# One matmul per key tile for the sums of V and K, in a backward pass of cached attention, with a new on-chip layout

## The chip, the cores and the metric

The kernel runs on one core of a Trainium2 chip. The metric is device time in microseconds, the median of several executions; all of them below are in the same (fast) state or, where a program ran once only, of unknown state. Ratios are the mean time of one kernel's runs over the mean of the other's runs of the same rounds, so they are not quite the ratio of the medians that are quoted. The kernel before has some stragglers: 5 of its 34 executions took 801.8 to 802.7 us, and no trace shows one.

## The reference, cut to what matters

One decode step of a small layer (attention over the last 4,096 keys of a cache of 32,768, then a gated feed-forward block) and its gradients with respect to every input.

```python
W = min(4096, max(256, Sk // 4))                       # 4096 keys used, 28672 not
k = jnp.repeat(k_cache[:, :, Sk - W:, :], rep, axis=1) # 8 heads of 256, 16 query heads
v = jnp.repeat(v_cache[:, :, Sk - W:, :], rep, axis=1)
p = _softmax(jnp.einsum("bhqd,bhkd->bhqk", q, k) * (Dh ** -0.5), axis=-1)
o = jnp.einsum("bhqk,bhkd->bhqd", p, v)
# outputs: the step's result and the gradients, among them those of the whole
# k_cache and v_cache, [1, 8, 32768, 256] in bfloat16 each, 268 MB together
```

Seven eighths of the two cache gradients are zero and must be written as zeros. That is what most of the kernel's bytes are.

## The kernel before

A 16 KB block of zeros per partition is sent again and again ("fills") to the untouched rows. The fills go out on the GpSimd queue in two batches. The second batch waits until the upper half of the zero block, which holds a block of feed-forward weights in between, is cleared again.

```python
HALF0, HALF1 = 42, 55          # 42 fills from 16 KB, 13 from its lower 8 KB read twice
send_fills(0, HALF0)
send_fills(HALF0, HALF1, True)
# ... cut: the attention forward stage, feed-forward blocks 0 and 1 ...
            if n == 1:
                nc.vector.memset(ar(ZW // 2, ZW // 2), 0.0)     # L426
                send_fills(HALF1, len(fills))                   # 48 more, from L427
```

In the forward stage each head g has its scores, then its "moments": the products p V^T K for the gradient of q (M_ps), and the sums of V and of K with the probabilities (ok_ps). These last are what the change touches:

```python
            for c in range(8):
                pK = pK_slot[c % 2]
                nc.vector.tensor_tensor(out=pK, in0=K_sb[:, 4*c:4*c+4, :]..., in1=p_f..., op=ALU.mult)   # L304
                for i in range(4):
                    for vh in range(2):
                        nc.tensor.matmul(M_ps[:, vh, :], lhsT=V_sb[:, t, ...], rhs=pK[:, i]...)          # L309
            for k, X_sb in enumerate((V_sb, K_sb)):
                for t in range(T):                                                                       # T = 32
                    nc.tensor.matmul(ok_ps[:, k, :], lhsT=ppad[...], rhs=X_sb[:, t, :], ...)             # L313
```

All big buffers are offsets in one arena: six regions of 16 KB for V, a region MB of 32 KB for the moments, and a region RB of 50 KB for K, the working slots and, after the stage, the output and feed-forward weights.

Of the kernel before, what the change touches and what calls it, by code (L numbers as in the profile page):

```python
# [15 lines left out]
H = 16  # L16
G = 8
Dh = 256
W = 4096
T = 32  # L20
# [9 lines left out]
KB = 512  # L30
# [3 lines left out]
def kernel(  # L34
        ctx, tc, A_x, A_k_cache, A_v_cache, A_wq, A_wo, B_x, B_w_gate, B_w_up, B_w_down, grad_out,
           out_0, out_1, out_2, out_3, out_4, out_5, out_6, out_7, out_8):
    nc = tc.nc
# [7 lines left out]
    ps_t = ctx.enter_context(tc.tile_pool(name="ps_t", bufs=1, space=bass.MemoryType.PSUM))  # L45

    VB = 16 * KB
    MB = VB + 6 * 16 * KB
    RB = MB + 32 * KB
    TOTAL = RB + 50 * KB  # L50
    arena = const.tile([128, TOTAL], bf16)

    def ar(off, n):
        return arena[:, off:off + n]

    def kv_at(off):
        return ar(off, T * Dh).rearrange("p (t d) -> p t d", d=Dh)

    zeros = ar(0, ZW)
    A_off = [VB + 16 * KB * i for i in range(6)]  # L60
    V_off = [A_off[i] for i in (0, 1, 2, 3, 4, 5, 0, 1)]
    K_off = [RB, RB + 16 * KB, MB + 16 * KB, RB, RB + 16 * KB, A_off[1], RB, RB + 16 * KB]
    M_sb = [ar(MB + 4 * KB * g, 4 * KB).bitcast(f32).rearrange("p (v h d) -> p v h d", v=2, h=2) for g in range(G)]
    wqA = ar(MB, 24 * KB).rearrange("p (c j) -> p c j", c=3)
    wqB = ar(MB + 24 * KB, 4 * KB)
    KT_slot = [ar(RB + (32 + 2 * i) * KB, 2 * KB).rearrange("p (e t k) -> p e t k", t=4, e=2) for i in range(3)]
    pK_slot = [ar(RB + (38 + 4 * i) * KB, 4 * KB).rearrange("p (t h d) -> p t h d", t=4, h=2) for i in range(2)]
    ppad = [ar(RB + (46 + i) * KB, T * H).rearrange("p (t h) -> p t h", h=H) for i in range(2)]
    rows1 = ar(RB + 48 * KB, 2 * KB)[0:16].bitcast(f32)
    ok_rows = ar(RB + 48 * KB, 2 * KB)[0:H].bitcast(f32).rearrange("p (k d) -> p k d", k=2)  # L70

# [123 lines left out]
    def load_kv(off, cache, g):  # L195
        LD.dma_start(out=kv_at(off), in_=cache[0, g, Sk - W:, :].rearrange("(p t) d -> p t d", t=T))
# [21 lines left out]
    for c in range(16):  # L218
        nc.tensor.matmul(qT_ps[:, c::16], lhsT=wqB[:, c * 128:(c + 1) * 128], rhs=X1_b[:, 3:5], start=True, stop=False)
        for h in range(2):  # L220
            col = 16 * h + c
            for k in range(3):
                nc.tensor.matmul(qT_ps[:, col:col + 1], lhsT=wqA[:, k, col * 128:(col + 1) * 128], rhs=X1_b[:, k:k + 1],
                                 start=False, stop=(h == 1 and k == 2))
# [14 lines left out]
    def fill_vpad(i, src):  # L239

        nc.vector.tensor_copy(out=vpad[i][:].rearrange("p e (c w) -> p e c w", w=18)[:, :, :, 0:2],
                              in_=src.unsqueeze(2).to_broadcast([128, 2, 8, 2]))
# [19 lines left out]
    with tc.tile_pool(name="ps_m", bufs=1, space=bass.MemoryType.PSUM) as ps_m, \  # L262
            tc.tile_pool(name="ps_x", bufs=1, space=bass.MemoryType.PSUM) as ps_x, \
            tc.tile_pool(name="ps_c", bufs=1, space=bass.MemoryType.PSUM) as ps_c, \
            tc.tile_pool(name="work1", bufs=2) as work1:

        def scores(g):
            fill_vpad(g % 2, qT_bf[:, 4 * g:4 * g + 4].rearrange("p (k e) -> p e k", e=2))
            sT_ps = dots(kv_at(K_off[g]), KT_slot, vpad[g % 2], rows1, ps_c, "cols", lambda q, XT, ps: nc.scalar.copy(out=XT, in_=ps))  # L269
            pmax = small.tile([16, 1], f32, tag="pmax")  # L270
            nc.vector.reduce_max(out=pmax[:], in_=rows1, axis=AX)
            pmaxT_ps = ps_t.tile([1, 16], f32, tag="tmp")
            nc.tensor.transpose(pmaxT_ps[:], pmax[:], ident_f[0:16, 0:16])
            gmax = small.tile([1, 2], f32, tag="gmax")
            nc.vector.reduce_max(out=gmax[:], in_=pmaxT_ps[:].rearrange("o (c h) -> o h c", h=2), axis=AX)
            nc.vector.tensor_scalar(out=gmax[:], in0=gmax[:], scalar1=-SCALE, scalar2=None, op0=ALU.mult)
            nb_ps = ps_t.tile([128, 2], f32, tag="tmp")
            nc.tensor.matmul(nb_ps[:], lhsT=ones_f[0:1, 0:128], rhs=gmax[:], start=True, stop=True)
            nbias = small.tile([128, 2], f32, tag="nbias")
            nc.vector.tensor_copy(out=nbias[:], in_=nb_ps[:])  # L280
            e_f = work1.tile([128, T, 2], f32, tag="e_f")
            psums = small.tile([128, 2], f32, tag="psums")
            for hh in range(2):
                nc.scalar.activation(out=e_f[:, :, hh], in_=sT_ps[:].rearrange("p i c h -> p (i c) h")[:, :, hh], func=ACT.Exp, bias=nbias[:, hh:hh + 1], scale=SCALE,  # L284
                                     accum_out=psums[:, hh:hh + 1])
            tot_ps = ps_t.tile([128, 2], f32, tag="tmp")
            nc.tensor.matmul(tot_ps[:], lhsT=ones_f[:, :], rhs=psums[:], start=True, stop=True)
            rsum = small.tile([128, 2], f32, tag="rsum")
            nc.vector.reciprocal(out=rsum[:], in_=tot_ps[:])
            nc.vector.tensor_tensor(out=pT_all[:, g], in0=e_f[:], in1=rsum[:].unsqueeze(1).to_broadcast([128, T, 2]), op=ALU.mult)  # L290
            p_f = work1.tile([128, T, 2], f32, tag="p_f")
            nc.vector.tensor_copy(out=p_f[:], in_=pT_all[:, g])
            pp = ppad[g % 2]
            if g > 1:
                nc.vector.memset(pp[:, :, 2 * g - 4:2 * g - 2], 0.0)
            nc.vector.tensor_copy(out=pp[:, :, 2 * g:2 * g + 2], in_=pT_all[:, g])  # L296
            return p_f

        def moments(g, p_f):
            K_sb, V_sb = kv_at(K_off[g]), kv_at(V_off[g])  # L300
            M_ps = ps_m.tile([128, 2, 2 * Dh], f32, tag="M")
            for c in range(8):
                pK = pK_slot[c % 2]
                nc.vector.tensor_tensor(out=pK, in0=K_sb[:, 4 * c:4 * c + 4, :].unsqueeze(2).to_broadcast([128, 4, 2, Dh]),  # L304
                                        in1=p_f[:, c::8, :].unsqueeze(3).to_broadcast([128, 4, 2, Dh]), op=ALU.mult)
                for i in range(4):
                    t = 4 * c + i
                    for vh in range(2):
                        nc.tensor.matmul(M_ps[:, vh, :], lhsT=V_sb[:, t, vh * 128:(vh + 1) * 128], rhs=pK[:, i, :, :].rearrange("p h d -> p (h d)"),  # L309
                                         start=(t == 0), stop=(t == T - 1))  # L310
            for k, X_sb in enumerate((V_sb, K_sb)):
                for t in range(T):
                    nc.tensor.matmul(ok_ps[:, k, :], lhsT=ppad[g % 2][:, 8 * (t % 4) + t // 4, :], rhs=X_sb[:, t, :],  # L313
                                     start=(g == 0 and k == 0 and t == 0), stop=(g == G - 1 and k == 1 and t == T - 1))
            for vh in range(2):
                nc.scalar.copy(out=M_sb[g][:, vh].rearrange("p h d -> p (h d)"), in_=M_ps[:, vh, :])

        def load_wo(n):
            LD.dma_start(out=wo_sb[:, 16 * n:16 * n + 16, :], in_=A_wo.rearrange("(p j) n -> p j n", j=32)[:, 16 * n:16 * n + 16, :])

        ok_ps = ps_x.tile([H, 2, Dh], f32, tag="ok")
        after = {0: [("K", 3), ("V", 3)], 1: [("K", 4), ("V", 4), ("K", 5)], 2: [("V", 5)], 3: [("V", 6), ("K", 6)], 4: [("K", 7)], 5: [("V", 7)]}
        p_next = scores(0)
        for g in range(G):
            p_f = p_next
            if g + 1 < G:
                p_next = scores(g + 1)
            moments(g, p_f)
            for kind, n in after.get(g, []):
                if kind == "K":  # L330
                    load_kv(K_off[n], A_k_cache, n)
                else:
                    load_kv(V_off[n], A_v_cache, n)
            if g == G - 2:
                load_wo(0)
        nc.vector.tensor_copy(out=ok_rows, in_=ok_ps[:])
# [151 lines left out]
    with tc.tile_pool(name="work2", bufs=2) as work2, tc.tile_pool(name="lnw", bufs=1) as lnw, \  # L488
            tc.tile_pool(name="ps_d", bufs=2, space=bass.MemoryType.PSUM) as ps_d:
        for g in range(G):  # L490
            dqb_ps = ps_d.tile([128, 2, 512], f32, tag="d", name="dqb_ps")
            for hh in range(2):
                h = 2 * g + hh
                for vh in range(2):
                    nc.tensor.matmul(dqb_ps[:, 0, hh * Dh:(hh + 1) * Dh], lhsT=doT_f[:, vh, h:h + 1].to_broadcast([128, 128]), rhs=M_sb[g][:, vh, hh, :],  # L495
                                     start=(vh == 0), stop=False)
                for kh in range(2):
                    nc.tensor.matmul(dqb_ps[:, 0, hh * Dh + kh * 128:hh * Dh + (kh + 1) * 128], lhsT=ndk[:, kh, h:h + 1].to_broadcast([128, 128]), rhs=ident_f[:],  # L498
                                     start=False, stop=(kh == 1))
            nc.scalar.activation(out=dq_bc[:, g * 512:(g + 1) * 512], in_=dqb_ps[:, 0, :], func=ACT.Copy, scale=SCALE)  # L500
        for g in range(2):
            load_kv(MB + 16 * KB * g, A_v_cache, g)

# [94 lines left out]
        for it, g in enumerate(order):  # L598
            V_sb = kv_at(V2_off[it])
# [31 lines left out]
            for l in range(8):  # L631
                for qp in range(2):
                    d_ps = ps_d.tile([128, 2, 2, Dh], f32, tag="d")
                    for qi in range(2):
                        q = 2 * qp + qi
                        nc.tensor.matmul(d_ps[:, qi].rearrange("p w d -> p (w d)"), lhsT=rT[32 * q:32 * (q + 1), :], rhs=RB_[32 * q:32 * (q + 1), l, :],  # L636
                                         start=True, stop=True)
                    t = 4 * l + 2 * qp
# [47 lines left out]
```

## Time and profile before

| | before |
|---|---|
| median of 3 executions before the prediction | 799.91 us |
| span of the profiled execution | 798.2 us |
| bytes moved by DMA | 334.80 MB, mean 419 GB/s |
| TensorE busy | 480.3 us, 3,159 instructions (some matmul records are missing: 489 of 512 at L309) |
| weight loads (PEld) busy | 245.3 us, 3,182 instructions |
| VectorE busy | 437.0 us |

A share of busy time is an average over stages. Here TensorE is 60% busy over the span and full in the forward stage, while the DMA engines are full everywhere but at the ends. The prediction below shows the lines. In the views PE is TensorE, PEld its weight loads, DVE VectorE, ACT ScalarE, POOL GpSimd and SPq the queue on which SyncE issues loads and stores; L numbers are lines of the kernel that ran, so they shift by some lines from one kernel to the next. The "hand-over" is the moment when the second batch of fills starts, the "backlog" what is left of the first batch until then.

### The profile page before, as it was taken

Reading aid. Unit: us, or ns where it says so; the run is one execution under the profiler, and the core shown is the slowest. Engines: PE = TensorE matmul, PEld = TensorE weight load, DVE = VectorE, ACT = ScalarE, POOL = GpSimd, SP = SyncE. Lnnn points to the kernel's source line nnn. Section 1 sums busy time; section 2 is a strip of 40 time slices with the busy share of each in tenths; the row PEclk is TensorE's granted clock in tenths of the full one; section 3 lists DMA queues with packets and bytes.
Section 4 is the critical chain, followed back from the end, with each engine's and each line's share of the span. In section 5 each row is a group of like instructions: output and inputs, shape, how many; then the busy total and the mean of one; then the engine's idle time right before and its main releaser. Section 6 shows DMA issues by size and latency. Waiting matters only on the chain.

```text
span 798.2 us, 7807 instructions
## 1 busy us (share of the span) xinstructions
PE 480.3 (60%) x3159; PEld 245.3 (31%) x3182; DVE 437.0 (55%) x629; ACT 195.9 (25%) x309; POOL 61.4 (8%) x112
## 2 busy tenths in 40 slices
PE   0459999999999998532309568683551542732000
PEld 0334545545445444311207434331210211310000
DVE  2116584765846783153791579579671894884000
ACT  0142314124132201000101117353330342444000
POOL 4000000010101110100210001010000000000000
PEclk9989999999999999555557869667555556675555
DMA  9999999999999999999999999999999999999995
GB/s 349 431 431 427 429 431 428 430 429 428 431 425 422 429 420 416 411 423 424 425 426 411 425 432 427 428 426 427 425 425 425 424 423 424 430 420 417 430 437 256
DMA packets 29354, 334.80 MB, mean 419 GB/s; under 512 B 2819, under 2 KB 5894, under 8 KB 7814
## 3 DMA queue, kind: packets, MB, share of 16 engines
q0 software_dynamic: 16496, 216.01, 64.0%
q1 hardware_dynamic: 11382, 116.68, 34.8%
q10 hardware_dynamic: 1440, 1.61, 0.6%
q8 instruction: 25, 0.41, 0.2%
q14 instruction: 11, 0.09, 0.0%
HBM read 53.69 MB, written 280.59 MB: 419 GB/s over the span
## 4 chain that ended last, share of the span: by engine, by line
DMA 47%; another core or an unknown queue 15%; DVE 14%; PE 9%; issue 3%; ACT 2%; POOL 1%; SPq 0%; DVEq 0%; ACTq 0%; POOLq 0%
DMA out_dram<-arena 47%; DVE arena L628 2%; DVE arena L452 2%; PE dqb_ps L495 2%; DVE arena L643 2%; PE rows_ps L255 2%; PE d_ps L636 2%; PE tr_ps L252 1%; DVE arena L644 1%; DVE arena L507 1%; POOL out_dram L132 1%; DVE arena L421 1%; PE dqb_ps L498 1%; DVE arena L537 1%
## 5 line engine op out<-in xcount | busy, mean ns | idle before, releaser
L304 DVE TENSOR_TENSOR arena<-arena,p_f 128x2048 bf16<-128x2048 bf16 x64 | 145.2, 2284 | 58.7 <-PE M_ps L309 58.6
L309 PE MATMUL M_ps<-arena 128*128 128x512 bf16 x489 | 126.4, 381 | 1.1
L636 PE MATMUL d_ps<-arena,rT 32*128 32x512 bf16 x256 | 46.9, 531 | 111.0 <-DVE arena L644 63.8
L252 PE MATMUL tr_ps<-ident_bf,arena 128*128 128x128 bf16 x1024 | 91.7, 241 | 18.8 <-ACT arena L604 11.3
L255 PE MATMUL rows_ps<-arena,vpad 128*16 128x512 bf16 x256 | 90.4, 451 | 20.6 <-DVE arena L606 14.6
L252 PEld LDWEIGHTS <-arena 128*128 128x128 bf16 x1024 | 68.4, 108 | 70.7 <-issue 62.7
L132 POOL DMA_DIRECT2D out_dram<-arena x90 | 48.2, 538 | 536.5 <-DMA out_dram<-arena 488.6
L269 ACT COPY arena<-tr_ps 128x1024 bf16<-128x1024 bf16 x64 | 61.8, 1015 | 68.3 <-PE tr_ps L252 68.3
L640 ACT CAST arena<-d_ps 128x512 bf16<-128x512 f32 x64 | 37.7, 589 | 129.5 <-PE d_ps L636 129.5
L313 PE MATMUL ok_ps<-arena 128*16 128x256 bf16 x512 | 64.5, 273 | 1.1 <-DVE arena L296 0.9
L309 PEld LDWEIGHTS <-arena 128*128 128x128 bf16 x512 | 43.3, 99 | 50.9 <-issue 15.2
L604 ACT COPY arena<-tr_ps 128x1024 bf16<-128x1024 bf16 x32 | 32.6, 1020 | 93.7 <-PE tr_ps L252 36.5
L636 PEld LDWEIGHTS <-rT 32*128 32x128 bf16 x256 | 11.3, 96 | 136.6 <-issue 90.4
L643 DVE CAST arena<-d_ps 128x512 bf16<-128x512 f32 x64 | 43.8, 684 | 17.1 <-PE d_ps L636 16.6
L313 PEld LDWEIGHTS <-arena 128*16 128x16 bf16 x512 | 41.9, 89 | 29.9 <-issue 21.0
L644 DVE CAST arena<-d_ps 128x512 bf16<-128x512 f32 x64 | 43.5, 679 | 10.6 <-DMA out_dram<-arena 10.6
L641 ACT CAST arena<-d_ps 128x512 bf16<-128x512 f32 x64 | 38.2, 596 | 11.3 <-DMA out_dram<-arena 11.3
L255 PEld LDWEIGHTS <-vpad 128*16 128x16 bf16 x256 | 19.4, 93 | 58.6 <-issue 51.6
L628 DVE TENSOR_TENSOR arena<-R_sb,tl_f 128x4096 bf16<-128x4096 bf16 x8 | 35.4, 4419 | 0.7 <-ACT R_sb L626 0.7
L507 DVE CUSTOM_DVE_ANT_0 arena<-arena 128x4096 bf16<-128x4096 bf16 x3 | 13.1, 4423 | 24.5 <-ACT arena L500 24.5
L284 ACT ACTIVATE e_f<-cols_ps,nbias 128x32 f32<-128x32 f32 x16 | 4.5, 286 | 85.7 <-DVE nbias L280 85.7
L257 DVE COPY arena<-rows_ps 16x512 f32<-16x512 f32 x16 | 10.8, 676 | 26.5 <-PE rows_ps L255 26.5
(198 smaller groups left out, 390.1 us busy)
## 6 DMA issues: line engine op xcount, KB each, us to landing
out_dram<-arena POOLq DMA_DIRECT2D x103, 2048.0 KB, 52.1
out_dram<-arena SPq DMA_DIRECT2D x18, 2048.0 KB, 32.6
arena<-in_A_v_cache_dram SPq DMA_DIRECT2D x10, 2048.0 KB, 49.2
arena<-in_A_k_cache_dram SPq DMA_DIRECT2D x8, 2048.0 KB, 29.4
out_dram<-arena SPq DMA_DIRECT2D x4, 4096.0 KB, 41.7
arena<-in_A_wq_dram SPq DMA_DIRECT2D x2, 3072.0 KB, 20.2
arena<-in_A_wo_dram SPq DMA_DIRECT2D x2, 1792.0 KB, 15.7
out_dram<-arena SPq DMA_DIRECT2D x2, 1792.0 KB, 15.6
```

Of the source, the lines that this page charges most:

```text
L132: ZQ.dma_start(out=reg, in_=zeros)
L252: nc.tensor.transpose(tr_ps[:, dh, i, :], X_sb[:, 4 * q + i, dh * 128:(dh + 1) * 128], ident_bf[:])
L255: nc.tensor.matmul(rows_ps[:], lhsT=pad[:, dh, 16 * q:16 * q + 16], rhs=XT[:, dh].rearrange("p t k -> p (t k)"), start=(q == 0 and dh == 0 ...
L269: sT_ps = dots(kv_at(K_off[g]), KT_slot, vpad[g % 2], rows1, ps_c, "cols", lambda q, XT, ps: nc.scalar.copy(out=XT, in_=ps))
L304: nc.vector.tensor_tensor(out=pK, in0=K_sb[:, 4 * c:4 * c + 4, :].unsqueeze(2).to_broadcast([128, 4, 2, Dh]), in1=p_f[:, c::8, :].unsqueez ...
L309: nc.tensor.matmul(M_ps[:, vh, :], lhsT=V_sb[:, t, vh * 128:(vh + 1) * 128], rhs=pK[:, i, :, :].rearrange("p h d -> p (h d)"), start=(t == ...
L313: nc.tensor.matmul(ok_ps[:, k, :], lhsT=ppad[g % 2][:, 8 * (t % 4) + t // 4, :], rhs=X_sb[:, t, :], start=(g == 0 and k == 0 and t == 0), ...
L628: nc.vector.tensor_tensor(out=RB_, in0=R_sb[:].unsqueeze(1).to_broadcast([128, 8, 512]), in1=tl_f[:].unsqueeze(2).to_broadcast([128, 8, 51 ...
L636: nc.tensor.matmul(d_ps[:, qi].rearrange("p w d -> p (w d)"), lhsT=rT[32 * q:32 * (q + 1), :], rhs=RB_[32 * q:32 * (q + 1), l, :], start=T ...
L641: nc.scalar.copy(out=stK[:, t:t + 2, :], in_=d_ps[:, :, 1, :])
L643: nc.vector.tensor_copy(out=stV[:, t:t + 2, :], in_=d_ps[:, :, 0, :])
L644: nc.vector.tensor_copy(out=stK[:, t:t + 2, :], in_=d_ps[:, :, 1, :])
```

## The change

The intent: the sum of V and the sum of K use the same stationary operand (lhsT, here the padded probabilities of a key tile), so one matmul with a moving operand (rhs) of 2 x 256 columns can do both. The two pieces of that operand are the V tile and the K tile, reached by one step in the access pattern. To keep that step small, the regions are laid out anew.

```diff
     VB = 16 * KB
-    MB = VB + 6 * 16 * KB
-    RB = MB + 32 * KB
-    TOTAL = RB + 50 * KB
+    RB = VB + 48 * KB
+    UB = RB + 50 * KB
+    MB = UB + 48 * KB
+    TOTAL = MB + 32 * KB
...
-    A_off = [VB + 16 * KB * i for i in range(6)]
+    A_off = [VB, VB + 32 * KB, UB + 32 * KB, UB, UB + 16 * KB, VB + 16 * KB]
-    K_off = [RB, RB + 16 * KB, MB + 16 * KB, RB, RB + 16 * KB, A_off[1], RB, RB + 16 * KB]
+    K_off = [RB, RB + 32 * KB, MB + 16 * KB, RB, RB + 32 * KB, A_off[1], RB, RB + 32 * KB]
...  (KT_slot, pK_slot and ppad move from RB + 32..48 KB to RB + 16..32 KB)
+        def both(g, t):
+            v, k = V_off[g] + t * Dh, K_off[g] + t * Dh
+            rhs = ar(v, Dh).unsqueeze(1).to_broadcast([128, 2, Dh])
+            steps = [list(d) for d in rhs.ap]
+            steps[1][0] = k - v
+            return bass.AP(tensor=rhs.tensor, offset=rhs.offset, ap=steps)
...
-            for k, X_sb in enumerate((V_sb, K_sb)):
-                for t in range(T):
-                    nc.tensor.matmul(ok_ps[:, k, :], lhsT=ppad[g % 2][:, 8 * (t % 4) + t // 4, :], rhs=X_sb[:, t, :],
-                                     start=(g == 0 and k == 0 and t == 0), stop=(g == G - 1 and k == 1 and t == T - 1))
+            for t in range(T):
+                nc.tensor.matmul(ok_ps[:].rearrange("p k d -> p (k d)"), lhsT=ppad[g % 2][:, 8 * (t % 4) + t // 4, :], rhs=both(g, t),
+                                 start=(g == 0 and t == 0), stop=(g == G - 1 and t == T - 1))
```

In the old layout, V and K of head 0 are 65,536 elements apart. In the new one the largest distance is 25,600. The Trainium skill ("SBUF — State Buffer", section "An operand's partitions come from dim 0 alone") says that a step of 32,768 elements does not fit its 16-bit field and fails at code generation.

More of the change, by code (lines that the diff above doesn't have):

```diff
@@ L65 @@
     wqB = ar(MB + 24 * KB, 4 * KB)
-    KT_slot = [ar(RB + (32 + 2 * i) * KB, 2 * KB).rearrange("p (e t k) -> p e t k", t=4, e=2) for i in range(3)]
-    pK_slot = [ar(RB + (38 + 4 * i) * KB, 4 * KB).rearrange("p (t h d) -> p t h d", t=4, h=2) for i in range(2)]
-    ppad = [ar(RB + (46 + i) * KB, T * H).rearrange("p (t h) -> p t h", h=H) for i in range(2)]
+    KT_slot = [ar(RB + (16 + 2 * i) * KB, 2 * KB).rearrange("p (e t k) -> p e t k", t=4, e=2) for i in range(3)]
+    pK_slot = [ar(RB + (22 + 4 * i) * KB, 4 * KB).rearrange("p (t h d) -> p t h d", t=4, h=2) for i in range(2)]
+    ppad = [ar(RB + (30 + i) * KB, T * H).rearrange("p (t h) -> p t h", h=H) for i in range(2)]
     rows1 = ar(RB + 48 * KB, 2 * KB)[0:16].bitcast(f32)
```

## The prediction

> **What bounds the kernel now.** I read the page's slices first, because a program of 334.80 MB may be bound by its transfers whatever its engines do. The rows are the busy tenths of TensorE, of the DMA engines, and the rate.
>
> ```profile
> PE   0459999999999998532309568683551542732000
> DMA  9999999999999999999999999999999999999995
> GB/s 349 431 431 427 429 431 428 430 429 428 431 425 422 429 420 416 411 423 424 425 426 411 425 432 427 428 426 427 425 425 425 424 423 424 430 420 417 430 437 256
> q0 software_dynamic: 16496, 216.01, 64.0%
> q1 hardware_dynamic: 11382, 116.68, 34.8%
> ```
>
> The DMA row has no hole: after the first slice it stays full until the last one. TensorE is full only from slice 4 to 15 and idles for the last three. Queue 0 is the zero-filling of the untouched cache gradient (216 MB); queue 1 is the loads and the computed outputs. So I then took the windows view in stretches of 20 us: time, PE busy, PEld, DVE, ACT, POOL, granted clock, DMA share, GB/s.
>
> ```profile
> 0.00:20.00 20.00, 0.37 (x1) 0.09 (x1) 4.55 (x18) 1.28 (x1) 9.39 (x18) 1.00 0.91 350
> 200.00:220.00 20.00, 19.95 (x114) 9.39 (x114) 17.54 (x17) 2.48 (x7) 2.13 (x4) 1.00 1.01 429
> 300.00:320.00 20.00, 15.50 (x99) 8.36 (x98) 7.09 (x19) 2.36 (x3) 2.00 (x3) 0.90 1.01 416
> 740.00:760.00 20.00, 0.00 (x0) 0.00 (x0) 0.00 (x0) 0.00 (x0) 0.00 (x0) 0.50 1.01 432
> 780.00:800.00 20.00, 0.00 (x0) 0.00 (x0) 0.00 (x0) 0.00 (x0) 0.00 (x0) 0.50 0.50 215
> ```
>
> The reader is to see three things. From 60 to 308 us, the attention forward stage with the changed matmuls, TensorE is the busiest engine (19.95 of 20), yet the DMA share is 1.01 beside it. From about 735 us no compute engine works any more, and transfers alone run for 60 us. Only the start and the last 20 us are below full rate. At 430 GB/s the bytes need 334.80 / 0.430 = 779 us, so even a perfect schedule would gain about 2.4% on the 798.2 us of the span, and what separates the two is the start, the tail and a few slices at 411 to 420. A faster engine repairs none of these.
>
> The one place where compute could reach the end is the hand-over between two batches of fills. The first (55 fills of 2 MiB) is issued early; the rest (48) waits for half of the zero buffer, which holds feed-forward weights in between. The POOL timeline and the wait view show it:
>
> ```profile
> 343.68 0.66 POOL L130 DMA_DIRECT2D out_dram<-arena  x1 [5.51 <-DMA out_dram<-arena]
> 380.73 3.68 POOL L132 DMA_DIRECT2D out_dram<-arena  x7 [36.39 <-DVE arena L426]
> POOL out_dram L132 <- DVE arena L426: 36.4, 1, 36.4
> ```
>
> POOL waits 36.4 us for the clearing at L426, but the DMA row shows no hole, so the backlog of the first batch covers it. Adding the packets of queue 0 in order, the 55 x 2 MiB = 115.3 MB are through at about 385 us, an estimate from the trace's packet records. So the hand-over has some 4 us of slack. More delay than that idles the DMA engines and costs the end microsecond for microsecond; an earlier hand-over brings nothing.
>
> **What the Trainium skill says.** In "TensorE: Matmul & The Clock Gate", section "Back-to-back issue gap", a warm matmul costs its moving columns over 2.4 GHz plus a fixed 2.5 ns: 262 cycles for 256 columns, 518 for 512. The stationary width is not in it. The trace roughly agrees: below, 112 ns for 256 columns against 109, and 229 ns for 512 against 216. The same page, "LDWEIGHTS (loading the stationary operand)", makes the weight load depend on its columns and "Step-by-step: what each phase is for" lets it run ahead of the current matmul; here L313's 16-column loads take a median 90 ns, less than the 112 ns of the matmul, so they hide. "DMA: Bandwidth & Descriptors", section "Where 436 GB/s comes from", gives a ceiling of 435 GB/s for the 16 engines; slices of 425 to 432 sit just under it. Section "Queues, rings and completion order" there says that each engine takes turns between queues by the packet, so loads beside the fills stretch: a 2 MiB key load has a median of 29.4 us in the issue table, some 5 us alone at 430 GB/s.
>
> **The change, part by part.** First the matmuls. The mean durations of the groups (273 ns at L313, 381 at L309) are pipelined times that overlap; the spacing is what counts. From the timeline of TensorE at the end of one head:
>
> ```profile
> 118.75 1.90 PE L309 MATMUL M_ps<-arena 128*128 128x512 bf16 x8
> 120.58 4.21 PE L313 MATMUL ok_ps<-arena 128*16 128x256 bf16 x37
> 124.72 0.45 PE L252 MATMUL tr_ps<-ident_bf,arena 128*128 128x128 bf16 x5
> ```
>
> Eight 512-column matmuls take 120.58 - 118.75 = 1.83 us, 229 ns each; 37 with 256 columns take 124.72 - 120.58 = 4.14 us, 112 ns each. The change removes 512 of the latter, 512 x 0.112 = 57.3 us, and adds 256 with twice the columns. Twice 112 is 224 ns (no saving), 229 is what the wide ones take here, and 217 is 224 less one saved start of the few ns above 256/2.4 = 107. The range is 256 x 0.217 to 0.229 = 55.6 to 58.6 us: between 1.7 us saved and 1.3 us lost out of a 250 us stage. The 256 weight loads saved are 256 x 90 ns = 23 us of PEld busy, all in the shadow. The intended gain, half the instructions, is almost no gain in time, as the columns are the same.
>
> Second, the operand. Its two 256-column halves are 16 to 50 KB apart. Each half is still contiguous, so I charge nothing for the jump. The dependencies must stay exact: a tracker that took everything between V and K as read would add waits. The gate and up loads of one block interleave in one region, and on the queues they are issued within 0.05 us of each other (308.66 and 308.71), though the gate needs 24.8 us to land. So interleaved strides are already told apart, and I expect no false wait.
>
> Third, the layout. K of heads 1, 4 and 7 moves from 16 KB to 32 KB into its region and changes places with the transpose slots, product slots and padded probabilities. What follows lies over other tenants. The SP queue before:
>
> ```profile
> 266.64 0.56 SPq L350 DMA_DIRECT2D arena<-in_B_w_gate_dram  x1
> 302.68 1.62 SPq L351 DMA_DIRECT2D arena<-in_B_w_down_dram  x2
> 307.79 0.33 SPq L319 DMA_DIRECT2D arena<-in_A_wo_dram  x1
> 308.66 2.50 SPq L349 DMA_DIRECT2D arena<-in_B_w_gate_dram  x2
> ```
>
> The two down-projection loads (1 MB) and the small gate piece lie after the change over K of head 7, free only when its last merged matmul ends, near 308: 5 and 42 us later. The second half of wo no longer lies over that K but over product slots, free when the M matmuls end near 304: up to 4 us earlier. The 1 MB at queue 1's pace there, about 5.6 MB in 40 us from the packet records, is 7 us moved from before wo to behind it or behind the first gate load. The chain to the hand-over runs wo, output row, its norm, up load of block 1, block 2's loads, clearing. So it may get shorter by some 4 us or longer by as much, within the slack or barely past it. In the backward stage the aliases among the six V regions, the M region and the R region are as before; I charge nothing.
>
> Sum: stage -1.7 to +1.3 us, hand-over -4 to +4 us, against 4 us of slack and a saturated DMA. On the end: 0, with perhaps +2 us in the unlucky corner. Bytes and packet sizes do not change.
>
> **Rivals.** (a) The stage is TensorE-bound and the change frees TensorE, so everything moves forward. For it: PE busy 19.95 of 20, and a naive reading of 64.5 us busy plus 41.9 us of weight loads at L313. Against it: the spacing above, and the DMA row. Even 20 us saved would only make the second batch queue earlier behind a backlog: 0 to -2 us. (b) The split moving operand streams slower, say 300 ns a matmul: 256 x 0.075 = 19 us more in the stage. Loads of later heads are far ahead, but the hand-over would slip 19 us, 15 past its slack, giving about 815 us. Against it: the product at L304 and the transposes at L252 already read strided views without trouble; nothing shows a two-piece matmul operand. (c) The later down-projection loads delay block 1 and 2 by 8 to 12 us: a DMA hole of 4 to 8 us around 385, giving 804 to 808. For it: DVE waits 12.8 us for gu of block 2 and TensorE 6.9 us for a gate load there, so that chain is bound by loads. (d) The layout shortens the chain to the hand-over: no change in time, only more slack.
>
> **Range and chances.** The three runs before span 799.44 to 802.68, and a reordered schedule changes the mix of reads and writes and how evenly the 16 engines end, some 2 us. Centre 799.5. The low end, 796, would need a better tail; the high end, 805, holds a DMA hole of 5 us. Faster by 2% would be 784, nearly the 779 of pure transfer: 0.01. Slower by 2% would be 816, which needs (b) in full: 0.03. The rest, 0.96.
>
> **What would show it.** Right: the ok matmul group with 256 instructions spaced 217 to 229 ns, forward stage ending within 3 us of 308, weight loads fewer by 256, DMA row full in every slice but the ends, bytes 334.80 MB, compute ended long before the last transfer. The down-projection loads would be issued near 308 rather than 302.68, wo near 304. Wrong: a spacing above 250 ns (then b); loads of K or V waiting for something that was not a wait before (false dependencies); a DMA slice under 9 near 385 (c); a faster end with a full DMA row, which would mean that the rate in GB/s, not the waits, had changed.

## The result, and the profile after

The changed kernel takes 798.95 us (798.60 to 799.07, 4 runs) against 799.87 us for the kernel before (4 runs). The ratio is 0.998 with a 95% interval from 0.9957 to 1.0003: the same within 2%, and inside the predicted range. A later set of five rounds gave 799.02 against 799.91 us, ratio 0.9982 (0.9967 to 0.9996). So some 0.9 us may be real; in the means the stragglers of the kernel before add to it.

The slices of the page after; the rows are TensorE, DMA, and the rate:

```profile
PE   0459999999999999251409478684450553722000
DMA  9999999999999999999999999999999999999995
GB/s 349 431 430 430 428 431 430 430 428 430 430 423 427 427 419 413 423 421 424 432 428 423 424 431 431 428 425 427 424 424 422 424 424 424 423 427 418 433 434 247
```

The DMA row is the same: full, except at the ends. The bytes are 334.76 MB (before: 334.80), the two queues' packets the same. The windows view, columns as in the prediction:

```profile
200.00:220.00 20.00, 20.00 (x91) 7.28 (x90) 17.66 (x17) 2.32 (x7) 1.89 (x4) 1.00 1.01 431
780.00:800.00 20.00, 0.00 (x0) 0.00 (x0) 0.00 (x0) 0.00 (x0) 0.00 (x0) 0.52 0.44 187
```

In the forward stage there are fewer instructions in the same time (91 matmuls in the stretch instead of 114), and TensorE is as full as before. At the end only transfers run, as before; the last 20 us move less because the end comes 1 us sooner.

TensorE at the end of the last head, from the timeline; first the line of the kernel before with which its stage ends, then the changed kernel:

```profile
308.56 0.96 PE L252 MATMUL tr_ps<-ident_bf,arena 128*128 128x128 bf16 x14
```

```profile
301.85 1.90 PE L317 MATMUL M_ps<-arena 128*128 128x512 bf16 x8
303.68 4.48 PE L320 MATMUL ok_ps<-arena 128*16 128x512 bf16 x20
308.09 0.95 PE L253 MATMUL tr_ps<-ident_bf,arena 128*128 128x128 bf16 x14
```

Twenty merged matmuls take 308.09 - 303.68 = 4.41 us, 220.5 ns each. 256 of them are 56.4 us, where 512 of 112 ns were 57.3: 0.9 us saved. The stage ends at 308.09 us instead of 308.56. Weight loads fell from 3,182 to 2,926, and PEld busy from 245.3 to 222.6 us, which nobody waited for.

The hand-over of the fills on the GpSimd queue, and the loads on the SP queue:

```profile
377.90 3.17 POOL L133 DMA_DIRECT2D out_dram<-arena  x6 [35.61 <-DVE arena L433]
```

```profile
299.58 0.56 SPq L357 DMA_DIRECT2D arena<-in_B_w_gate_dram  x1
302.96 0.33 SPq L326 DMA_DIRECT2D arena<-in_A_wo_dram  x1
307.98 0.38 SPq L356 DMA_DIRECT2D arena<-in_B_w_gate_dram  x1
308.40 1.18 SPq L358 DMA_DIRECT2D arena<-in_B_w_down_dram  x2
```

The second batch starts at 377.90 us instead of 380.73. The second half of wo is issued 4.8 us sooner (302.96 against 307.79), the two down-projection loads 5.7 us later (308.40 against 302.68). The VectorE timeline shows what the later loads do, in the first product that needs them, before and after:

```profile
311.69 0.63 DVE L396 CUSTOM_DVE_ANT_0 arena<-arena,dh_bc 128x448 bf16<-128x448 bf16 x1
329.94 0.62 DVE L403 CUSTOM_DVE_ANT_0 arena<-arena,dh_bc 128x448 bf16<-128x448 bf16 x1 [18.72 <-DMA arena<-in_B_w_down_dram]
```

VectorE stands for 18.72 us waiting for the down-projection weights, and the output row behind it comes at 333.17 instead of 330.22 us. That the hand-over is nevertheless earlier goes, in the trace, with another order on VectorE: it now does block 0's weight products (L428) before it copies block 1's gate and up products out of PSUM (L411, for which it waited 9.32 us in the kernel before), so block 2's gate load is issued at 350.12 instead of 353.81 us.

### The profile page after: what moved, and what is told of

It reads as the page before. It is cut to its first block, busy times and chain, and to the rows that moved or that the text cites. A ratio compares the mean times of both kernels' runs of the same rounds, so it can differ in the third digit from the quotient of the medians.

```text
span 797.2 us, 7318 instructions
## 1 busy us (share of the span) xinstructions
PE 478.9 (60%) x2926; PEld 222.6 (28%) x2926; DVE 437.1 (55%) x629; ACT 196.0 (25%) x309; POOL 61.8 (8%) x112
## 2 busy tenths in 40 slices
DMA packets 29352, 334.76 MB, mean 420 GB/s; under 512 B 2819, under 2 KB 5894, under 8 KB 7814
## 4 chain that ended last, share of the span: by engine, by line
PE 37%; DMA 32%; DVE 16%; ACT 4%; issue 2%; another core or an unknown queue 0%; SPq 0%; DVEq 0%; ACTq 0%
DMA out_dram<-arena 19%; PE M_ps L317 12%; PE ok_ps L320 7%; PE rows_ps L256 6%; PE tr_ps L253 4%; DMA dh_bc<-in_grad_out_dram 4%; DMA arena<-in_A_k_cache_dram 4%; DMA arena<-in_B_w_down_dram 3%; ACT arena L270 2%; DVE arena L635 2%; DVE arena L459 2%; PE dqb_ps L502 2%; DMA arena<-in_B_w_gate_dram 2%; DVE arena L650 2%; PE d_ps L643 2%
## 5 line engine op out<-in xcount | busy, mean ns | idle before, releaser
L317 PE MATMUL M_ps<-arena 128*128 128x512 bf16 x512 | 128.9, 380 | 0.2 <-ACT arena L323 0.2
L320 PE MATMUL ok_ps<-arena 128*16 128x512 bf16 x256 | 63.8, 381 | 0.9 <-DVE arena L297 0.9
L317 PEld LDWEIGHTS <-arena 128*128 128x128 bf16 x512 | 43.3, 99 | 59.0 <-issue 23.2
L320 PEld LDWEIGHTS <-arena 128*16 128x16 bf16 x256 | 19.1, 89 | 41.6 <-issue 20.5
```

What stands on the lines that cost most here:

```text
L317: nc.tensor.matmul(M_ps[:, vh, :], lhsT=V_sb[:, t, vh * 128:(vh + 1) * 128], rhs=pK[:, i, :, :].rearrange("p h d -> p (h d)"), start=(t == ...
L320: nc.tensor.matmul(ok_ps[:].rearrange("p k d -> p (k d)"), lhsT=ppad[g % 2][:, 8 * (t % 4) + t // 4, :], rhs=both(g, t), start=(g == 0 and ...
```

## The experiments

The theory: the end is the sum of the bytes over a saturated rate, and compute can touch it only where the second batch of fills comes too late ("transfer theory"). The rival: the forward stage is bound by TensorE and sets the end, and the change did little because it saved little ("TensorE theory"). Eleven runs were made, one of them the changed kernel again. All edits are against the changed kernel unless said otherwise.

### The yardstick

No edit.

> The changed kernel once more, as the yardstick of these runs. Transfer theory (the end is the sum of bytes over a saturated rate): 798.5 to 799.5 us, ratio to before 0.998 to 1.000. TensorE theory (the forward stage sets the end, the change saved a little of it): the same, as the stage ends only 0.5 us earlier; this run alone does not tell them apart.

Measured: correct, 799.02 us (5 runs); before 799.91 us in these rounds (11 runs). As expected.

### Take TensorE work away

```diff
-            for t in range(T):
+            for t in range(0, T, 2):
```

> The changed kernel with the merged matmul on even key tiles only (wrong sums on purpose): 128 of 256 gone, 128 x 0.221 us = 28 us less TensorE work in a stage where TensorE is busy without a gap. TensorE theory: the end 28 us earlier, 771 us, or at least 10 us. Transfer theory: 798 to 799.5 us, with the stage ending 20 to 28 us earlier (about 282) and the DMA row full.

Measured: 798.75 us (4 runs; sums wrong), ratio to before 0.9987 (0.9972 to 1.0002). The end of the stage in its TensorE timeline:

```profile
280.85 1.06 PE L253 MATMUL tr_ps<-ident_bf,arena 128*128 128x128 bf16 x16
```

Its hand-over in the POOL timeline:

```profile
369.95 2.65 POOL L133 DMA_DIRECT2D out_dram<-arena  x5 [25.03 <-DVE arena L433]
```

The stage ends at 280.85 us, 27 us before the changed kernel's 308.09, and the hand-over is 8 us earlier. The end moves by 0.3 us. Saving 30 times what the change saved gives nothing, so the smallness of the saving is not why the change is neutral. The rival falls.

### Add TensorE work, with and without the hand-over

```diff
+                for rr in range(2):                       # each merged matmul twice
```

> The changed kernel with each merged matmul issued twice (sums doubled, wrong on purpose): 256 x 0.221 = 57 us more TensorE work. TensorE theory: 57 us later, 856 us. Transfer theory with the hand-over slack of about 6 us: the first batch of fills runs dry at about 385 or somewhat earlier, the second cannot start before about 430, so a hole in the DMA row and an end 35 to 50 us later, 834 to 849 us.

Measured: 830.67 us (4 runs; wrong), 31.7 us over the changed kernel. That is less than either theory said. The slices of this run:

```profile
DMA  9999999999999999993199999999999999999997
GB/s 352 431 431 430 429 430 428 429 432 429 419 431 415 430 399 423 426 420 150 56 386 411 420 428 430 431 429 425 423 426 423 424 424 423 431 420 421 436 430 321
```

Its hand-over in the POOL timeline:

```profile
414.76 4.21 POOL L133 DMA_DIRECT2D out_dram<-arena  x8 [85.32 <-DVE arena L434]
```

For the first time the DMA row has a hole, in slices 19 and 20. The stage ends 55 us later (363.4 us), but the hand-over only 36.9 us later. The trace shows where the chain behind the stage got shorter: the down-projection loads are issued at 358.77 us, before the stage ends, so the output row comes 9.6 us after that end (373.05) instead of 25.1; and block 2's gate load, issued at 396.80 into the hole, is used at 403.60, 6.8 us later instead of 16.7 (350.12 to 366.85). Of the 36.9 us 31.7 reach the end. The rest is little backlog: the rate falls to 279 GB/s from 378 to 379 us and to 34 from 380 to 381, at most 3 us after the changed kernel's hand-over at 377.90. But other transfers still moved 7, 110 and 65 GB/s in the three stretches of 10 us from 380 to 410, which at 428 GB/s would have taken 4.3 us. The mechanism was right; the estimate of the hole had left out the shorter chain and these transfers.

Now the same doubling, with all fills in one batch that never waits (HALF1 = 103, all from the lower half of the zeros):

> The same doubled matmuls, with all fills in one batch that never waits. TensorE theory: still 57 us later, 856 us. Transfer theory: the hole is gone, 798 to 802 us, although the forward stage ends 57 us later; compute would end near 790 instead of 735, still before the last transfer.

And that batch alone, without the doubling:

> The changed kernel with all 103 fills in one batch, read from the half of the zero buffer that is never overwritten, so that the fills never wait for the feed-forward weights. Transfer theory: no gain, 798 to 800 us, since the hand-over had 4 to 6 us of slack. If the hand-over was costing time after all: faster, by up to the hole, 2 to 5 us. If fills that read the same 8 KB twice are slower by themselves: slower, 805 or more.

Measured: 801.76 us with the doubling (4 runs, wrong) and 801.69 us without it (6 runs, correct). The lines with which the stage ends, without and with the doubling:

```profile
306.80 0.95 PE L253 MATMUL tr_ps<-ident_bf,arena 128*128 128x128 bf16 x14
```

```profile
363.45 0.96 PE L253 MATMUL tr_ps<-ident_bf,arena 128*128 128x128 bf16 x14
```

This is the cleanest result: 57 us of added TensorE work in a full TensorE stage cost 0.07 us once the fills do not depend on it (the two were measured in different rounds, in which the kernel before had 799.92 and 799.91 us). VectorE's last instruction starts at 738.6 us with the doubling and at 692.0 without. My expectation of 790 was wrong: I had added the 57 us to the 735 us of the kernel before, but with one batch compute ends at 692 (in the changed kernel at 731.7), and the doubling moved it by 47 us.

The one batch itself is slower than two, 801.69 against 799.02 us, just outside what was expected. The trace offers a cause: 35,497 packets against 29,352. That is 6,145 more, and 48 more fills that send two pieces for each of 128 partitions make 6,144. In the stretch from 400 to 640 us this run moves 421 GB/s, the changed kernel 426. Over these 240 us that is 1.2 MB, 2.8 us at 428 GB/s. No run varied the packet size alone, so this is a reading of the trace and not a separate test.

### Take bytes away

Three of the late 4 MiB fills are not sent (rows left unwritten, wrong):

```diff
-late_jobs = [(out_2, G - 1, 5, 7, 2 * ZW), (out_3, G - 1, 0, 6, 2 * ZW), (out_3, G - 1, 6, 7, ZW)]
+late_jobs = [(out_2, G - 1, 5, 7, 2 * ZW), (out_3, G - 1, 6, 7, ZW)]
```

> The changed kernel without three of the last fills of 4 MiB, 12.58 MB that are left unwritten (wrong on purpose, unless the buffer was zero). They are sent after all compute is over. Transfer theory: 12.58 / 0.428 = 29 us less, 770 us (768 to 772). TensorE theory: no change on the stage; but as the fills are last, it cannot explain 29 us either, only their own latency of 44 us once, of which the fourth remains: 795 or more.

Measured: 770.14 us (4 runs), 28.9 us less than the yardstick, where 29 were expected. Its page:

```profile
DMA packets 28920, 322.18 MB, mean 419 GB/s; under 512 B 2771, under 2 KB 5846, under 8 KB 7766
```

Next a correct kernel with fewer bytes. V of head 0 is loaded twice, once for each pass. Keeping the moments in bfloat16 frees 16 KB; V of head 6 goes there, so V of head 0 stays. Head 6 is then too far from its K for one step and keeps two matmuls.

```diff
-M_sb = [ar(MB + 4 * KB * g, 4 * KB).bitcast(f32)...]
+M_sb = [ar(MB + 2 * KB * g, 2 * KB)...]
-V_off = [A_off[i] for i in (0, 1, 2, 3, 4, 5, 0, 1)]
+V_off = [A_off[i] for i in (0, 1, 2, 3, 4, 5)] + [MB + 16 * KB, A_off[1]]
-        for g in range(2):
-            load_kv(MB + 16 * KB * g, A_v_cache, g)
+        load_kv(MB, A_v_cache, 1)
-order = [2, 3, 4, 5, 6, 7, 0, 1]
+order = [2, 3, 4, 5, 0, 7, 6, 1]
...  (the product with M_sb takes doT_bf instead of doT_f)
```

> The changed kernel with V of head 0 kept on chip instead of loaded twice (the moments are kept in bfloat16 to make the room; V of head 6 takes the room, head 6 keeps two matmuls). 2.10 MB fewer bytes. Transfer theory: 2.10 MB at 0.428 MB per us is 4.9 us less, so 794 us (793 to 795.5), ratio 0.993. TensorE theory or any theory in which the backward stage's compute sets the end: 799 us, as that load was hidden beside compute. Correct within the tolerance is expected.

Measured: correct, 794.36 us (5 runs), ratio to before 0.9925 (0.991 to 0.994).

```profile
DMA packets 29209, 332.67 MB, mean 420 GB/s; under 512 B 2804, under 2 KB 5879, under 8 KB 7799
```

The bytes fell by 334.76 - 332.67 = 2.09 MB, 4.9 us at 0.428 MB per us, and the time by 799.02 - 794.36 = 4.7 us. This is the fastest correct kernel. The order of the heads and the type of the moments changed with it, but the bytes account for the gain.

### The layout without the merge

```diff
-            for t in range(T):
-                nc.tensor.matmul(ok_ps[:].rearrange("p k d -> p (k d)"), ..., rhs=both(g, t), ...)
+            for k, X_sb in enumerate((V_sb, K_sb)):
+                for t in range(T):
+                    nc.tensor.matmul(ok_ps[:, k, :], ..., rhs=X_sb[:, t, :], ...)
```

> The new layout with the two old matmuls per key tile. If the matmuls gave the 0.9 us: 799.9 us, as before. If the layout gave it (hand-over of the fills at 377.9 instead of 380.7 us): 799.0 us, as after. Transfer theory: between 798.5 and 800.5 in either case, TensorE 0.7 us later at the stage's end, the DMA row full. The two 256-column matmuls stay at 112 ns each, weight loads at 512.

Measured: correct, 801.00 us (6 runs, 800.25 to 802.78; the profiled one was the 802.78). Both guesses missed: layout alone is slower than the changed kernel (799.10 at most). Against the kernel before it is not clear of the noise (ratio 1.0011, 0.9995 to 1.0027). Its hand-over in the POOL timeline:

```profile
385.98 4.20 POOL L133 DMA_DIRECT2D out_dram<-arena  x8 [43.01 <-DVE arena L434]
```

Its windows from 380 to 390 us:

```profile
380.00:385.00 5.00, 0.00 (x0) 0.00 (x0) 4.58 (x8) 0.00 (x0) 0.00 (x0) 0.50 0.56 236
385.00:390.00 5.00, 2.04 (x6) 0.58 (x7) 4.90 (x16) 1.01 (x1) 4.02 (x8) 0.50 0.68 272
```

The changed kernel in the same windows:

```profile
380.00:385.00 5.00, 2.65 (x19) 2.06 (x19) 3.39 (x10) 1.77 (x3) 1.60 (x4) 0.50 1.02 436
385.00:390.00 5.00, 0.69 (x2) 0.10 (x1) 3.65 (x6) 0.76 (x2) 0.53 (x1) 0.50 1.02 438
```

Here the hand-over is past the slack, and the DMA share falls to 0.56. Against 428 GB/s the two windows lost 1.7 MB, 4.1 us, and this execution took 3.8 us more than the changed kernel; the others, without a trace, took 1.2 to 3.0 us more. The later down-projection loads of the new layout hold VectorE until 333.09 us. In this kernel VectorE then waits for block 1's gate and up products before block 0's weight products (L429 at 354.97 us, against 345.77 in the changed kernel), so block 2's gate load is issued at 359.32 us instead of 350.12. The two kernels differ in the merge alone, yet the scheduler, which orders the instructions when the program is built, chose another order for VectorE. It is here the order of the kernel before, whose hand-over was at 380.73: in that order, the new layout comes with a hand-over 5.3 us later. So what the traces show to differ between this kernel and the changed one is the order and the hole behind it; the stage itself ends 1.3 us later here (309.37).

Whether the hole is the whole difference was tested by more backlog, HALF1 = 59 instead of 55 in this same kernel:

> The new layout with the two old matmuls, and 59 instead of 55 fills in the first batch. Layout alone measured 801.0 us, with a hand-over at 386 us and the DMA rate down to 236 to 272 GB/s from 380 to 390 us. If that hole is all that separates it from the changed kernel: four more fills are some 20 us more backlog (2.10 MB each at 0.428 MB per us), the hole closes, and it measures 799.0 to 799.6 us, like the changed kernel. If the two old matmuls cost time in another way: it stays at 801.

Measured: correct, 799.91 us (5 runs), with a hand-over at 386.09 us and a rate of 428 and 429 GB/s in the same two windows. The hole is closed and 1.1 us are gone. The 0.9 us that remain to the changed kernel are a little more than expected, and the time is that of the kernel before (ratio 0.9997). Four more half fills mean 512 more packets, which at the cost seen in the one batch (2.7 us for 6,145) would be 0.2 us; the rest is not explained.

The converse on the changed kernel, HALF1 = 52:

> The changed kernel with 52 instead of 55 fills in the first batch. The backlog then ends some 15 us sooner, near 370 us, with the hand-over near 377: a hole of some 7 us opens, and the end comes 4 to 7 us later, 803 to 806 us, although not one instruction of the compute changes. If the hand-over does not matter: 799 us.

Measured: correct, 808.57 us (5 runs), ratio to before 1.0106. Windows of this run:

```profile
365.00:370.00 5.00, 3.25 (x37) 2.91 (x37) 0.26 (x2) 0.00 (x0) 0.00 (x0) 0.50 0.52 217
370.00:375.00 5.00, 0.00 (x0) 0.00 (x0) 4.65 (x9) 0.00 (x0) 0.00 (x0) 0.50 0.02 7
375.00:380.00 5.00, 2.03 (x5) 0.57 (x6) 4.83 (x13) 0.00 (x0) 2.88 (x6) 0.50 0.39 157
```

The same compute, three fills fewer in front, and the end is 9.6 us later. Against 428 GB/s these three windows lost 5 us x (211 + 421 + 271) GB/s = 4.5 MB, or 10.5 us. I had expected a hole of 7 us; the backlog ran dry between 367 and 368 us rather than at 370 (336, 188 and 106 GB/s in the three microseconds from 366), and the first bytes of the second batch moved 1 us after its issue at 377.12 (0 GB/s from 377 to 378, then 508). The effect is as the theory says, its size was underrated.

### The jump in the moving operand

```diff
-rhs=both(g, t)
+rhs=ar(V_off[g] + min(t, T - 2) * Dh, 2 * Dh)      # two neighbouring V tiles, no jump
```

> The merged matmul with 512 neighbouring columns of V (two key tiles side by side) in place of one tile of V and one of K far apart: same count, same columns, no jump in the moving operand, wrong sums on purpose. If the jump costs nothing: 220 to 222 ns from one to the next, as with the jump. If the jump costs something: shorter, about 216. Time 798 to 800 either way.

Measured: 798.58 us (one look; wrong on purpose). Its last sums:

```profile
304.55 4.48 PE L320 MATMUL ok_ps<-arena 128*16 128x512 bf16 x20
308.97 0.95 PE L253 MATMUL tr_ps<-ident_bf,arena 128*128 128x128 bf16 x14
```

4.42 us for twenty, 221 ns each, the same as with the jump of up to 50 KB. The jump costs nothing that can be seen.

## Why the prediction was right

**The bound.** Right, and tested from both sides: 27 us less TensorE time gave 0.3 us, 57 us more gave 0.07 us where the fills did not wait for it, and bytes removed came back at 0.43 to 0.45 MB per us (12.58 MB for 28.9 us, 2.09 MB for 4.7 us).

**The matmuls.** The spacing, 220.5 ns, lies in the predicted 217 to 229, and the stage's gain in the predicted band (0.5 us of at most 1.7). Rival (a) is refuted by the halved sums, rival (b) by the spacing itself, with the joined operand as a check. The weight loads hid, but the dependence on columns that the prediction took from the skill is hardly there in the trace: loads of 16 columns took 89 ns (L320), loads of 128 columns 99 ns (L317).

**The dependencies.** No load of K or V gained a wait that moved the stage: it ends 0.5 us earlier. The exact tracking went further than I had used it. I had the small gate piece wait for the last merged matmul, "42 us later", near 308. It was issued at 299.58, 33 us later: it lies over only a few tiles of K of head 7, and those are free early. That step took a region as one unit where it is many.

**The layout and the hand-over.** The sum was right (2.8 us earlier, predicted -4 to +4), but its chain was incomplete. I had written that the chain runs over wo and the output row. In the changed kernel it runs over the down-projection loads, as the products that need them stand before the output row in VectorE's order of instructions (18.72 us of waiting). Rival (c) therefore did happen, in layout_only, and cost 2.0 us against the changed kernel in the median and 3.8 in the execution with a trace, where the prediction had 4 to 8; in the changed kernel another order on VectorE made up for it. That the sum still fell into the range was luck. I had not counted on the scheduler's order changing, and no run forced the order by itself.

**The slack.** Its sign was right, its size was not. Hand-overs at 377.9 and 380.7 us left no hole, one at 386.0 did. But the estimate took the end of the last packet of the first batch (385), and the rate falls earlier: in layout_only the rate is 385 GB/s from 381 to 382 us, 238 in the next microsecond and 90 in the one after, in double_sums it falls from 378 on, and in after_less_first it fell 2 to 3 us before its estimate. If that holds for the kernel before, whose fills and loads are the same bytes, its hand-over at 380.73 had about 1 us of slack and not 4. Whether its slow executions of 802 us are those that crossed the line is not shown.

**Still open.** The 0.9 us between before and after. They are not the stage's TensorE time, since halved sums brought only 0.3 us more. The rate between 300 and 400 us is 423 GB/s after and 420 before, which would be 0.7 us, but no run isolates why. Nearly half of that lies beside the hand-over, from 380 to 390 us (421 and 425 GB/s before, 436 and 438 after), which would fit a hand-over with hardly any slack; it is not tested.

## What to carry to other kernels

Look at the DMA row before the engine that is busiest: in a stage where both are full, as here, less work on the engine only brings forward its wait for the transfers. Merging two matmuls into one of the same total columns saved instructions and weight loads here, and only 0.9 of 57 us of streaming time; the 22.7 us of weight loads that went had been hidden. Where a backlog covers a wait, find out how long it covers it, from when the rate falls and not from the last packet, because a layout or an order that moves the wait by a few us can cross that line; after_less_first crossed it without a change in any compute instruction. What moved the end otherwise was bytes.

## What the Trainium skill lacked or had wrong

- "TensorE: Matmul & The Clock Gate", section "Back-to-back issue gap": for streams of a weight load and a matmul it gives a sustained spacing of about 131 ns at 512 columns and calls the formula of columns over 2.4 GHz plus 2.5 ns (216 ns) an over-count. Here such streams with operands of 128 rows run at 220.5 ns (16-column weights) and 229 ns (128-column weights), not near 131; the formula is the better guide. At 256 columns it gives 109 ns, the trace 112.
- The same page has no statement on a moving operand in two far pieces: 220.5 ns with the jump, 221 ns without.
- "DMA: Bandwidth & Descriptors", section "Where 436 GB/s comes from", says that for transfers between HBM and on-chip memory a limit of about 358 GB/s binds, although it names a measurement of 425 GB/s beside it. On this one core, 281 of 334 MB being writes, 428 GB/s held from 20 to 300 us and 434 from 740 to 780 us, at the other limit of that page (435), and the mean over the span was 420. "Perfetto Trace Analysis", section "Roofline", has it right for a core alone.
- I found no page that compares large packets on this chip: a fill in two pieces per partition instead of one went with 421 instead of 426 GB/s and 2.7 us on the whole (one_batch), untested by itself.
